# Four blocks of 448 tokens in layer 1, and 512s and 384s in layer 2, of an attention and two-layer MLP kernel

## The chip, the cores and the metric

The kernel runs on one core of one Trainium2 chip. The metric is the device time of one execution in microseconds, the median of several runs. Before the change it is 988.56 us (three runs, 987.62 to 990.99).

## What is computed

Attention over q, k and v of shape (4, 8, 576, 64), as the sum of two parts, then two dense layers over the 2304 tokens with 512 features each:

```python
q_d, k_d, v_d = (t.reshape(B, H, 144, 4, D).mean(axis=3) for t in (q, k, v))
out_up = np.repeat(sm_attn(q_d, k_d, v_d), 4, axis=2)
scores = np.where(abs(pos[:, None] - pos[None, :]) < 4, q @ k.T / 8, -1e9)
x = (out_up + softmax(scores) @ v), as (2304, 512)
h = x @ moe_w_in;   y = (h * sigmoid(1.702 * h)) @ moe_w_out
h = y @ moe2_w_in;  out = where(h > 0, h, exp(min(h, 0)) - 1) @ moe2_w_out
```

The four weight matrices are 512 x 2048 or 2048 x 512 and come as 64-bit floats.

## The kernel before, in words

Every large product is made of three: each operand is split into a high and a low part of the type fp32r, and high x high, high x low and low x high are added up in PSUM.

**Weights.** A layer has 32 weight tiles, `wi0` to `wi15` (the 16 column blocks of w_in) and `wo0` to `wo15` (the 16 row blocks of w_out). `load_w` (L129, the DMAs of L136 and L141 on SP's queue) brings one tile of 512 KB, 64-bit numbers. `conv_w` turns it into high and low parts: ACT L158, DVE L165 (twice, or once and ACT L168 for some tiles of layer 1), DVE L171, ACT L178 (the high part), DVE L182 (the low part). `Weights.convert` (L222) does one call's worth: the low part of one tile, the high part of another, the first half of a third. `need` (L234) forces conversions that are not yet done when a tile is about to be used.

**Layer 1** takes the tokens in the blocks of BLOCKS1. `tiles_of(blk)` is 512 // columns, so a block of 256 columns takes two of the 16 tiles of w_in a step (8 steps), a block of 512 one (16 steps). A step is `products_h1` (L755, 12 matmuls for each of its tiles, then the chain ACT L776 tanh, DVE L779, ACT L780 high part, DVE L781 low part) and, two steps later (LAG), `products_y1` (L789, 12 matmuls per tile into the y tiles in PSUM). On a block's last step the y tiles are copied out by ACT L810 into places of the tag `g`, of which there are two and which h's chain uses too, and stored to `ydram` by SP (L811): four `ye` tiles for a block of 512, two for one of 256. From block 2 on, a new block first splits its x (L299, L300), then finishes the y steps that wait, then begins with three h's. There are two places in PSUM for h.

**Attention** is cut into pieces that stand in a queue; `attend` (L727) emits one. In the loop over the steps (L994) one piece follows each chunk of matmuls (four a step), and a block whose inputs are not ready takes pieces until they are (L997).

**Layer 2** takes blocks of 512 tokens, the last of 256. Step s is `hidden2` (L935): 12 matmuls of `products_h2`, the chain ACT L921, ACT L922, DVE L924, ACT L929, DVE L931, one `convert` and on every fourth step a second. `products_o2` (L954) for the step two earlier follows: for each 128 tokens three matmuls of 512 columns. The first two steps of layer 2 stand beside the last two y steps of layer 1. On a block's last step ACT L970 and DVE L972 copy o out and SP stores it (L973). The rows of y of the next block are loaded by `load_y` (L887) and split by `split_y` (L892) in steps 8 to 13.

**Layer 2's weights.** After step 0 of the last block of layer 1 the attention's memory is free and the second `Weights` begins (L1056). Its first six tiles have places of their own; the others take the places of layer 1's tiles in the order of `released` (L982), as these have been read for the last time: `used` names the places that are free. In the last block of layer 1 a step calls `convert` once after its second chunk, and once more after its third chunk when the step's number is odd (L1030). Steps are counted from 0; the last block has the numbers 64 to 71. Its step 1 has two chunks, the steps from 2 on four.

Of the kernel before, what the change touches and what calls it, by code (L numbers as in the profile page):

```python
# [26 lines left out]
NF = 16  # L27
NK = 4
NSUM = 4

BLOCKS1 = [(0, 256), (256, 256), (512, 512), (1024, 512), (1536, 512), (2048, 256)]

XBUFS = 2
NEG = -1.0e9
# [21 lines left out]
LAG = 2  # L56
# [10 lines left out]
def kernel(  # L67
# [23 lines left out]
    NT = B * S  # L91
    NBLK = len(BLOCKS1)
    PSUM = bass.MemoryType.PSUM
# [162 lines left out]
    @contextmanager  # L256
    def behind():
        with ExitStack() as stack:
            for ins in urgent.values():
                stack.enter_context(tc.issue_after(ins.ins))  # L260
            yield
# [19 lines left out]
    def x_tile(blk):  # L281
        if blk not in x32:
            x32[blk] = xin.tile([P, NK, BLOCKS1[blk][1]], F32, tag="x32", name=f"x32_{blk}", bufs=XBUFS)
        return x32[blk]

    def block_of(gw):

        return next(i for i, (t0, n) in enumerate(BLOCKS1) if t0 <= 64 * gw < t0 + n)

    def split_x(blk, c):  # L290
        if blk not in xsplit:

            n = BLOCKS1[blk][1]
            nb = 2 if blk == 0 else 1
# [12 lines left out]
    class Unit:  # L307
# [284 lines left out]
        def pv(self, w0, w1):  # L592
# [10 lines left out]
            while a < w1:  # L603
                gw = self.b * NWIN + a
                blk = block_of(gw)
                t0, n = BLOCKS1[blk]
                e = min(w1, a + (t0 + n) // 64 - gw)
# [116 lines left out]
    def ready(blk):  # L724
        return not due[blk]

    def attend():  # L727

        if deferred:
            deferred.pop(0)()  # L730
        if not queue:
            return False
        piece, ends = queue[0]
        if ends is not None and block_of(ends.b * NWIN + ends.w1 - 1) >= nsplit[0] // NK + XBUFS:
            return False
        queue.pop(0)
        piece()
        if ends is not None:
            for users in due.values():
                users.discard(ends)  # L740
        return True

    def split_some(blk):

        if blk < NBLK and nsplit[0] < NK * (blk + 1) and ready(blk):
            split_x(blk, nsplit[0] % NK)
            nsplit[0] += 1
# [3 lines left out]
    def tiles_of(blk):  # L751

        return 512 // BLOCKS1[blk][1]

# [34 lines left out]
    def products_y1(blk, st):  # L789
        nf, (t0, tb) = tiles_of(blk), BLOCKS1[blk]  # L790

        if st == 0:
            yps[blk] = [ypool.tile([P, nf, tb], F32, tag=f"y{i % 2}", name=f"y{i}_{blk}") for i in range(NK // nf)]
        gh, gl = hg.pop((blk, st))
        last = st == NF // nf - 1
        for m in range(NK):
            n = 0
            for i in range(nf):
                f = nf * st + i
                for wp, gp in ((0, gh), (0, gl), (1, gh)):  # L800
                    nc.tensor.matmul(  # L801
                        out=yps[blk][m // nf][:, m % nf, :],
                        lhsT=w_out(1, f, wp)[:, m, :], rhs=gp[:, i, :],
                        start=(st == 0 and n == 0 and m % nf == 0), stop=(last and n == 3 * nf - 1),
                        skip_group_check=True,
                    )
                    n += 1
            if last and m % nf == nf - 1:
                t = gpool.tile([P, nf, tb], F32, tag="g", name=f"ye{m // nf}_{blk}", bufs=2)
                nc.scalar.activation(out=t, in_=yps[blk][m // nf], func=AF.Copy, scale=0.5)  # L810
                nc.sync.dma_start(  # L811
                    out=ydram[m - nf + 1:m + 1, :, t0:t0 + tb].rearrange("c p t -> p c t"), in_=t
                )
            if m % 2 == 1:
                yield
# [30 lines left out]
    kd, f = spare.pop(0)  # L846
# [30 lines left out]
        steps += [catch.pop(0), ahead.pop(0)]  # L877
    steps += catch + [(blk, st) for blk in range(2, NBLK) for st in range(NF // tiles_of(blk))]

    blocks = [(t, min(512, NT - t)) for t in range(0, NT, 512)]  # L880
    steps2 = [(bi, f) for bi in range(len(blocks)) for f in range(NF)]
    x2 = {}
    y32 = {}
# [3 lines left out]
    def load_y(bi, c):  # L887
        t0, n = blocks[bi]
        y32[bi, c] = x2pools[0].tile([P, 512], F32, tag="y32", name=f"y32_{bi}_{c}", bufs=2)
        nc.sync.dma_start(out=y32[bi, c][:, :n], in_=ydram[c, :, t0:t0 + n])  # L890
# [44 lines left out]
    def hidden2(s):  # L935
        bi, f = steps2[s]
        wt2.need("i", f)
        low_part = products_h2(s)
        if bi + 1 < len(blocks):
            if 8 <= f < 8 + NK:  # L940
                load_y(bi + 1, f - 8)
            if 10 <= f < 10 + NK:
                split_y(bi + 1, f - 10)
        wt2.load(AHEAD + wt2.half - wt2.loaded)
        with behind():
            wt2.convert()
        low_part()
        if s % 4 == 3:
            with behind():
                wt2.convert()  # L950
# [24 lines left out]
    wt2 = None  # L975
# [4 lines left out]
    order2 += [("o", f) for f in range(NF - 4, NF)]  # L980

    released = []  # L982
    for f2 in range(8 + LAG):
        released += [f"wi{f}" for f in (2 * f2, 2 * f2 + 1) if f < NF]
        released += [f"wo{f}" for f in (2 * (f2 - LAG), 2 * (f2 - LAG) + 1) if f >= 0]
    used = set()

    def rate(si):
        if due[1] and si < 8:
            return RATE0  # L990
        return RATE1

    waiting, prev = [], None
    for si, (blk, f2) in enumerate(steps + [(None, None)] * LAG):  # L994
        chunks = []
        if blk is not None:
            while not ready(blk):  # L997
                assert attend()
            if blk > 1 and f2 == 0:

                for _ in range(NK):
                    split_some(blk)
                while waiting:
                    prev = waiting.pop(0)
                    wt1.need("o", tiles_of(prev[0]) * (prev[1] + 1) - 1)
                    chunks.append(products_y1(*prev))
            while nsplit[0] < NK * (blk + 1):
                split_some(blk)
            wt1.need("i", tiles_of(blk) * (f2 + 1) - 1)
            chunks.append(products_h1(blk, f2))  # L1010
            waiting.append((blk, f2))
            if blk == NBLK - 1:
                used |= {f"wi{2 * f2}", f"wi{2 * f2 + 1}"}
        if len(waiting) > LAG or blk is None:
            prev = waiting.pop(0)
            wt1.need("o", tiles_of(prev[0]) * (prev[1] + 1) - 1)
            chunks.append(products_y1(*prev))
        if blk is None:
            hidden2(si - len(steps))
        nchunk = 0  # L1020
        for chunk in chunks:
            for _ in chunk:
                if not wt1.finished() and blk == 0:
                    wt1.convert()
                for _ in range(rate(si)):
                    attend()
                if blk == 0:
                    split_some(1)
                nchunk += 1
                if wt2 is not None and nchunk in (2, 3) and (nchunk == 2 or si % 2):  # L1030
                    wt2.load(AHEAD + wt2.half - wt2.loaded)
                    with behind():
                        wt2.convert()
        if blk == NBLK - 1:
            if 1 <= f2 <= NK:
                load_y(0, f2 - 1)
            if 3 <= f2 < 3 + NK:
                split_y(0, f2 - 3)
        if chunks and prev is not None and prev[0] == NBLK - 1:
            used |= {f"wo{2 * prev[1]}", f"wo{2 * prev[1] + 1}"}  # L1040
        if wt1.finished() and stage1 is not None:
            ls1.close()
            stage1 = None
        if not queue and nsplit[0] == NK * NBLK and l1a is not None:
            l1a.close()
            l1x.close()
            l1s.close()
            hpools.append(ls2.enter_context(tc.tile_pool(name="hpool2", bufs=2, space=PSUM, side="right")))
            l1a = None
            stage2 = ls2.enter_context(tc.tile_pool(name="stage2", bufs=1, side="right"))  # L1050
            x2pools.append(ls2.enter_context(tc.tile_pool(name="x2a", bufs=1, side="right")))
            wextra = ls2.enter_context(tc.tile_pool(name="wextra", bufs=1, side="right"))
            for i, tile2 in enumerate(order2):
                places[(2, *tile2)] = (wextra, f"we{i}") if i < NEXTRA else (wpool, released[i - NEXTRA])
            used |= {f"we{i}" for i in range(NEXTRA)}
            wt2 = Weights(2, order2, stage2, 3, lambda tag: tag in used, 0)  # L1056
            wt2.load(AHEAD)
# [9 lines left out]
    for s in range(LAG, len(steps2) + LAG):  # L1067
        if s < len(steps2):
            hidden2(s)
        f = steps2[s - LAG][1]  # L1070
# [34 lines left out]
```

## Time and profile before

| | |
|---|---|
| median of three runs | 988.56 us |
| profiled execution, span from first to last instruction | 1196.4 us (no other time of it is given) |
| granted TensorE clock of that execution, mean | 0.750 |
| matmuls (PE) busy | 1183.7 us, 99% |
| DVE busy | 503.3 us, 42% |
| ACT busy | 471.7 us, 39% |
| POOL busy | 102.0 us, 9% |

One execution is profiled; its span is longer than the runs that were only timed. PE is TensorE's matmuls, PEld its weight loads, DVE is VectorE, ACT ScalarE, SP the engine whose queue issues most DMAs. A row of a group of instructions gives line, engine, operation, tiles (out<-in), shape and count, then busy time in us, the mean of one in ns, and idle time before them with what ended it. In the order of time a row gives start and duration in us, and in brackets the idle time before it. Matmul durations overlap, so the pace is read from starts. `L766` and `L801` are h and y of layer 1, `L914` and `L963` h and o of layer 2.

### The profile page before, as it was taken

What the parts mean: (1) busy time and instruction counts of PE and PEld (TensorE: products, weight loads), DVE (VectorE), ACT (ScalarE), POOL (GpSimd) and SP (SyncE); (2) the same over time, 40 slices, a digit from 0 to 9 for tenths busy, and PEclk for the clock granted to TensorE, in tenths of its full rate; (3) what the DMA queues carried; (4) which work ended last, traced back from release to release, by engine and by line L of the source; (5) the groups of instructions that cost most, each with busy time, mean ns of one, the idle gap of its engine ahead of it and who ended that gap; (6) DMA issues with size and microseconds to landing.
All of it is one profiled execution on the core that took longest, in us unless ns stands there. A gap on an engine that the chain in (4) does not pass through costs nothing.

```text
span 1196.4 us, 15208 instructions
## 1 busy us (share of the span) xinstructions
PE 1183.7 (99%) x6028; PEld 881.7 (74%) x6028; DVE 503.3 (42%) x898; ACT 471.7 (39%) x1116; POOL 102.0 (9%) x117
## 2 busy tenths in 40 slices
PE   9999999999999999999999999999999999999998
PEld 4578999976667677777668986677767777676787
DVE  3777785344453442122122796673213222221222
ACT  5888654233332441122113464553223222322233
POOL 4243210211230000000000000000000000000000
PEclk8777777776777777777777777777777777777777
DMA  9668612332331102100004940001001000100000
GB/s 194 157 157 225 145 27 39 68 58 34 47 52 23 43 16 74 44 3 33 1 1 128 315 156 0 1 14 58 1 1 35 27 1 1 44 0 1 1 36 18
DMA packets 128822, 68.04 MB, mean 57 GB/s; under 512 B 99184, under 2 KB 118768, under 8 KB 128752
## 3 DMA queue, kind: packets, MB, share of 16 engines
q1 hardware_dynamic: 109040, 63.21, 18.9%
q0 software_dynamic: 14976, 2.69, 2.7%
q10 hardware_dynamic: 4736, 1.18, 0.6%
q8 instruction: 47, 0.77, 0.3%
q14 instruction: 23, 0.19, 0.1%
HBM read 57.59 MB, written 9.44 MB: 56 GB/s over the span
## 4 chain that ended last, share of the span: by engine, by line
PE 97%; ACT 2%; DVE 1%; issue 0%; DVEq 0%; ACTq 0%
PE h L766 22%; PE y L801 21%; PE o L963 21%; PE h L914 20%; PE busy L853 3%; PE qk L468 2%; PE pv L598 2%; PE ptr L572 2%; PE qkd L495 1%; PE pvd L582 1%; PE pdt L560 1%; PE pt L421 1%; ACT pd L525 0%; DVE wst1i L165 0%; ACT sl L518 0%
## 5 line engine op out<-in xcount | busy, mean ns | idle before, releaser
L801 PE MATMUL y<-g1h,whl1o 128*128 128x256 f32 (+1 forms) x768 | 253.3, 401 | 0.0
L963 PE MATMUL o<-whl2o,g2h 128*128 128x512 f32 x576 | 214.1, 457 | 0.0
L766 PE MATMUL h<-xh,whl1i 128*128 128x256 f32 (+1 forms) x768 | 209.6, 406 | 0.3 <-ACT xh L299 0.3
L914 PE MATMUL h<-x2h,whl2i 128*128 128x512 f32 (+1 forms) x640 | 190.9, 427 | 0.0
L801 PEld LDWEIGHTS y<-g1h,whl1o 128*128 128x128 f32 x768 | 154.6, 217 | 35.6 <-issue 3.4
L766 PEld LDWEIGHTS h<-xh,whl1i 128*128 128x128 f32 x768 | 143.1, 219 | 35.2 <-issue 3.0
L924 DVE SCALAR_TENSOR_TENSOR g<-e,h 128x512 f32<-128x512 f32 (+1 forms) x80 | 50.7, 634 | 262.8 <-ACT e L922 262.6
L914 PEld LDWEIGHTS h<-x2h,whl2i 128*128 128x128 f32 x640 | 122.9, 201 | 45.6
L801 PE MATMUL y<-g1l,whl1o 128*128 128x256 f32 (+1 forms) x384 | 152.5, 397 | 0.0
L963 PEld LDWEIGHTS o<-whl2o,g2h 128*128 128x128 f32 x576 | 113.7, 199 | 46.5
L921 ACT ACTIVATE e<-h 128x512 f32<-128x512 f32 (+1 forms) x80 | 44.5, 556 | 252.2 <-PE h L914 252.2
L963 PE MATMUL o<-whl2o,g2l 128*128 128x512 f32 x288 | 131.7, 457 | 0.0
L776 ACT ACTIVATE g<-h 128x512 f32<-128x512 f32 x72 | 42.8, 596 | 202.2 <-PE h L766 200.6
L779 DVE SCALAR_TENSOR_TENSOR g<-g,h 128x512 f32<-128x512 f32 x72 | 49.1, 685 | 174.4 <-ACT g L776 174.4
L766 PE MATMUL h<-xl,whl1i 128*128 128x256 f32 (+1 forms) x384 | 107.5, 403 | 0.0
L380 POOL DMA_DIRECT2D vd<-in_v_dram x72 | 84.7, 1238 | 243.0 <-DMA vd<-in_v_dram 181.0
L914 PE MATMUL h<-x2l,whl2i 128*128 128x512 f32 (+1 forms) x320 | 95.7, 427 | 0.0
L801 PEld LDWEIGHTS y<-g1l,whl1o 128*128 128x128 f32 x384 | 83.8, 218 | 15.1 <-issue 0.3
L766 PEld LDWEIGHTS h<-xl,whl1i 128*128 128x128 f32 x384 | 72.9, 224 | 15.4 <-issue 2.0
L914 PEld LDWEIGHTS h<-x2l,whl2i 128*128 128x128 f32 x320 | 61.1, 201 | 21.7
L963 PEld LDWEIGHTS o<-whl2o,g2l 128*128 128x128 f32 x288 | 57.6, 200 | 23.9
L931 DVE TENSOR_TENSOR g2l<-g,g2h 128x512 fp32r<-128x512 f32 (+1 forms) x80 | 51.6, 645 | 36.7 <-ACT g2h L929 36.2
(110 smaller groups left out, 1185.6 us busy)
## 6 DMA issues: line engine op xcount, KB each, us to landing
wst1i<-in_moe_w_in_dram SPq DMA_DIRECT2D x16, 512.0 KB
wst1o<-in_moe_w_out_dram SPq DMA_DIRECT2D x16, 512.0 KB
wst2i<-in_moe_w_in_dram SPq DMA_DIRECT2D x16, 512.0 KB
wst2o<-in_moe_w_out_dram SPq DMA_DIRECT2D x16, 512.0 KB
ydram<-ye SPq DMA_DIRECT2D x18, 256.0 KB
out_dram<-ot SPq DMA_DIRECT2D x18, 256.0 KB
y<-ydram SPq DMA_DIRECT2D x16, 256.0 KB
vw<-in_v_dram SPq DMA_DIRECT2D x24, 122.5 KB
```

Of the source, the lines that this page charges most:

```text
L380: nc.gpsimd.dma_start(out=self.vd[:, :, j, :], in_=src, accum_op=ALU.add)
L468: nc.tensor.matmul(out=ps[r, w - a, :], lhsT=self.qkT[0][r, 64 * w:64 * w + 64], rhs=self.qkT[1][r, ks:ks + KW], start=not by_pe, stop=Tru ...
L766: nc.tensor.matmul(out=ph[:, i, :], lhsT=w_in(1, f, c, wp), rhs=xp[:, c, :], start=(n == 0), stop=(n == 3 * NK - 1),)
L776: nc.scalar.activation(out=g, in_=ph, func=AF.Tanh, scale=0.851)
L779: nc.vector.scalar_tensor_tensor(out=g, in0=g, scalar=1.0, in1=ph, op0=ALU.add, op1=ALU.mult)
L801: nc.tensor.matmul(out=yps[blk][m // nf][:, m % nf, :], lhsT=w_out(1, f, wp)[:, m, :], rhs=gp[:, i, :], start=(st == 0 and n == 0 and m % ...
L853: ins = nc.tensor.matmul(out=busy.rearrange("p a b -> p (a b)")[:, :n], lhsT=ones[:, :P], rhs=ones[:, :n], start=True, stop=True)
L914: nc.tensor.matmul(out=ph[:, :n], lhsT=w_in(2, f, c, wp), rhs=xp[:, c, :n], start=(i == 0), stop=(i == 3 * NK - 1),)
L921: nc.scalar.activation(out=e[:, :n], in_=ph[:, :n], func=AF.Relu, scale=-1.0)
L924: urgent["dve"] = nc.vector.scalar_tensor_tensor(out=g[:, :n], in0=e[:, :n], scalar=-1.0, in1=ph[:, :n], op0=ALU.add, op1=ALU.max)
L931: return lambda: nc.vector.tensor_tensor(out=gl[:, :n], in0=g[:, :n], in1=gh[:, :n].bitcast(F32), op=ALU.subtract)
L963: nc.tensor.matmul(out=ops[bi][i], lhsT=gp[:, i * P:(i + 1) * P], rhs=wo[wp], start=(f == 0 and m == 0), stop=(f == NF - 1 and m == 2),)
```

## The change

The last four blocks of layer 1 have 448 columns each in place of 512, 512, 512 and 256; layer 2 has three blocks of 512 and two of 384 in place of four of 512 and one of 256. As `tiles_of(448)` is 1, the last block of layer 1 has 16 steps of one tile and not 8 of two, so the places of layer 1's weights come free one `wi` and one `wo` a step, and `convert` is called once a step there, never twice.

```diff
-BLOCKS1 = [(0, 256), (256, 256), (512, 512), (1024, 512), (1536, 512), (2048, 256)]
+BLOCKS1 = [(0, 256), (256, 256), (512, 448), (960, 448), (1408, 448), (1856, 448)]
+BLOCKS2 = [(0, 512), (512, 512), (1024, 512), (1536, 384), (1920, 384)]
...
-    blocks = [(t, min(512, NT - t)) for t in range(0, NT, 512)]
+    blocks = BLOCKS2
...
-    for f2 in range(8 + LAG):
-        released += [f"wi{f}" for f in (2 * f2, 2 * f2 + 1) if f < NF]
-        released += [f"wo{f}" for f in (2 * (f2 - LAG), 2 * (f2 - LAG) + 1) if f >= 0]
+    for st in range(NF + LAG):
+        released += [f"wi{st}"] if st < NF else []
+        released += [f"wo{st - LAG}"] if st >= LAG else []
...
             if blk == NBLK - 1:
-                used |= {f"wi{2 * f2}", f"wi{2 * f2 + 1}"}
+                used.add(f"wi{f2}")
...
-                if wt2 is not None and nchunk in (2, 3) and (nchunk == 2 or si % 2):
+                if wt2 is not None and nchunk == 2:
                     wt2.load(AHEAD + wt2.half - wt2.loaded)
                     with behind():
                         wt2.convert()
...
         if chunks and prev is not None and prev[0] == NBLK - 1:
-            used |= {f"wo{2 * prev[1]}", f"wo{2 * prev[1] + 1}"}
+            used.add(f"wo{prev[1]}")
```

## Rows read from the trace of the kernel before

**Rows 1.** The page: busy time of the engines, granted clock by slice, chain that ended last

```profile
PE 1183.7 (99%) x6028; PEld 881.7 (74%) x6028; DVE 503.3 (42%) x898; ACT 471.7 (39%) x1116; POOL 102.0 (9%) x117
...
PEclk8777777776777777777777777777777777777777
...
PE 97%; ACT 2%; DVE 1%; issue 0%; DVEq 0%; ACTq 0%
```

**Rows 2.** Stages of the span (columns in the first line)

```profile
core 0: us, PE busy (x) PEld busy (x) DVE busy (x) ACT busy (x) POOL busy (x), PEclk, DMA share, GB/s
...
294.00:430.00 136.00, 136.00 (x805) 93.62 (x805) 59.01 (x115) 47.34 (x159) 20.33 (x18) 0.75 0.21 38
...
539.00:648.00 109.00, 109.00 (x386) 76.38 (x385) 24.64 (x38) 24.00 (x42) 0.00 (x0) 0.75 0.05 15
648.00:713.00 65.00, 65.00 (x423) 62.01 (x422) 50.04 (x79) 34.72 (x60) 0.00 (x0) 0.75 0.78 262
713.00:820.00 107.00, 107.00 (x379) 74.95 (x378) 70.76 (x113) 53.67 (x90) 0.00 (x0) 0.75 0.04 10
820.00:1131.00 311.00, 311.00 (x1098) 217.90 (x1097) 70.47 (x106) 91.61 (x151) 0.00 (x0) 0.75 0.04 14
```

**Rows 3.** PE in order of time, 1131 to 1134 us

```profile
1131.36 0.74 PE L914 MATMUL h<-x2h,whl2i 128*128 128x256 f32 x4
...
1133.06 0.74 PE L963 MATMUL o<-whl2o,g2h 128*128 128x512 f32 x2
...
1133.91 0.74 PE L963 MATMUL o<-whl2o,g2h 128*128 128x512 f32 x2
```

**Rows 4.** PE in order of time, 685.4 to 685.7 us, single matmuls of 256 columns

```profile
685.38 0.32 PE L801 MATMUL y<-g1h,whl1o 128*128 128x256 f32 x1
685.50 0.32 PE L801 MATMUL y<-g1l,whl1o 128*128 128x256 f32 x1
685.65 0.47 PE L801 MATMUL y<-g1h,whl1o 128*128 128x256 f32 x2
```

**Rows 5.** Groups of DVE instructions, 648 to 713 us

```profile
L165 DVE TENSOR_SCALAR wst2i<-wst2i 128x512 uint16<-128x512 uint16 x18 | 13.5, 762 | 0.1
L165 DVE TENSOR_SCALAR wst2o<-wst2o 128x512 uint16<-128x512 uint16 x10 | 7.6, 756 | 0.0
L171 DVE SCALAR_TENSOR_TENSOR ww2i<-ww2i,wst2i 128x512 int32<-128x512 int32 x8 | 5.6, 706 | 0.4
L182 DVE TENSOR_TENSOR whl2i<-ww2i,whl2i 128x512 fp32r<-128x512 f32 x8 | 5.6, 705 | 0.0
```

**Rows 6.** PE in order of time, 787 to 791 us

```profile
787.49 1.32 PE L963 MATMUL o<-whl2o,g2h 128*128 128x512 f32 x4
...
790.90 0.47 PE L963 MATMUL o<-whl2o,g2h 128*128 128x512 f32 x1
```

**Rows 7.** DVE in order of time, 789 to 818 us

```profile
789.59 0.68 DVE L182 TENSOR_TENSOR whl2o<-ww2o,whl2o 128x512 fp32r<-128x512 f32 x1
...
816.84 0.69 DVE L182 TENSOR_TENSOR whl2o<-ww2o,whl2o 128x512 fp32r<-128x512 f32 x1
```

**Rows 8.** Two stretches of layer 2's first block, columns as in rows 2

```profile
695.60:716.40 20.80, 20.80 (x100) 16.83 (x99) 20.13 (x34) 14.73 (x26) 0.00 (x0) 0.75 0.50 175
716.40:800.00 83.60, 83.60 (x297) 58.58 (x296) 55.64 (x89) 40.81 (x69) 0.00 (x0) 0.75 0.00 0
```

**Rows 9.** All engines in order of time, entries into the fifth and sixth block

```profile
539.75 1.09 ACT L810 ACTIVATE ye<-y 128x512 f32<-128x512 f32 x2 [1.67 <-DMA ydram<-ye]
...
647.93 0.74 PE L766 MATMUL h<-xh,whl1i 128*128 128x256 f32 x4
...
653.24 0.69 DVE L779 SCALAR_TENSOR_TENSOR g<-g,h 128x512 f32<-128x512 f32 x1
```

**Rows 10.** Waits, 300 to 475 us: the longest of PE and its weight loads

```profile
PEld pv L598 <- issue: 2.9, 6, 0.5
```

**Rows 11.** SP's queue in order of time, the last loads of layer 2's weights

```profile
695.35 1.97 SPq L141 DMA_DIRECT2D wst2o<-in_moe_w_out_dram  x4
```

## The prediction, made before the changed kernel was built or run

> **What bounds the kernel now.** I read the page first, then stages, then single instructions. The page [rows 1] shows TensorE (PE) busy 99% of a 1196.4 us span, the chain that ended last 97% on PE, and a granted clock of 6 to 8 tenths of 2.4 GHz in every slice (0.75 in all stages of [rows 2]), between its two levels of 1.2 and 2.4 GHz. By stage [rows 2] PE has no idle time in any stretch shown, while DVE and ACT are busy a quarter to three quarters. The pace of single matmuls [rows 3] says what PE is short of. In layer 2's last block, twelve 256-column matmuls start at 1131.36 and the next ones at 1133.06: 142 ns each. Three 512-column ones take 1133.91 - 1133.06 = 0.85 us: 283 ns each. Twice the columns, twice the time: in this execution PE is bound by columns alone, with nothing fixed per matmul.
>
> **The timed runs are another case.** The only time known of the profiled execution is its span; the median of the runs shown, 988.56 us, is 208 us shorter. The four large products (h and y of layer 1, h and o of layer 2) each move 2304 x 192 = 442,368 columns, 1.769 million in all; at 283 ns for 512 they take 978 us. The rest of the profiled span, 218 us, could not fit into the 11 us that 988.56 would leave, so the timed runs had a faster PE. If only the products ran faster, they had 771 us, a clock of about 0.95; if all shrank alike, 0.75 x 1196.4 / 988.56 = 0.91; with any stall in them, more, up to 1. DVE, ACT and DMA have the durations of the rows in both cases. So I make two sums: against the profiled execution, and against PE at 2.4 GHz, where the covers shrink to 0.75 of themselves.
>
> **Columns and matmul counts.** Layer 1 keeps six blocks of 192 h and 192 y matmuls, layer 2 five blocks of 192 h, and o depends on no block size. Columns and counts stay: 0 in the profiled execution. What goes are 384 + 192 = 576 matmuls of 256 columns (the sixth block of layer 1, h of the fifth of layer 2). At 2.4 GHz they could lie above their 107 ns, should the weight load beside each not fit. Lower end: proportional as in [rows 3], 0. Upper end: single 256-column matmuls start as near as 120 ns and 150 ns to each other [rows 4]; the short one would leave 13 ns, 576 x 13 = 7.5 us. The pace of [rows 3] is the mean of many, [rows 4] a pair, so I take 1 us gained. The Trainium skill (TensorE: Matmul & The Clock Gate, section "LDWEIGHTS (loading the stationary operand)") has a load cost its columns at 1.2 GHz, 107 ns for 128: an estimate that just fits under a 256-column matmul, so by it this term is 0 and the sum below 1 us smaller; no row here shows a load as the limit.
>
> **Conversions started before layer 2 (the main term).** Each weight tile costs DVE two L165, one L171 and one L182: 2 x 0.76 + 0.71 + 0.70 = 2.93 us [rows 5]. By the code, before: step 0 of the sixth block opens the conversion; steps 1 to 7 give one call each, steps 3, 5 and 7 a second, the two steps with layer 2's first h two each: 14 ([rows 5] have 28 L165, 14 tiles). Then steps 2 to 15 give 14 + 4 = 18: the 32nd comes exactly at the block's end. After: 15 + 4 = 19 before, so the 32nd comes at step 11. What that is worth at present: the last tiles are ready just in time. PE turns from h to o at 787.49 and wants a low part at 790.90 [rows 6]; that part's DVE instruction starts at 789.59 and lasts 0.68 [rows 7], ready at 790.27. From the end of h it took 2.78 us (ACT's two passes, DVE's two), under a cover of twelve matmuls, 3.41 us. The profiled execution gains 0. At 2.4 GHz the cover is 2.56 us, 0.22 short, some 0.25 with a semaphore; six tiles (the last at 816.84 [rows 7]) stand so: 1.5 us stall now, gone after, since the tiles are four steps early. If the clock is 0.92 or less it is 0.
>
> **DVE's backlog.** From 695.6 to 716.4, where layer 2's first h stands beside the last y, DVE is busy 20.13 of 20.80 us [rows 8]. At 2.4 GHz PE passes this in 15.6: DVE comes out 4.5 us late. The next stretch has 55.64 us of DVE work in 83.6, at 2.4 GHz in 62.7, so up to 7 us to catch up, if DVE need not idle for ACT. Bounds 0 and 4.5; I take half, 2.3 us now. After, the same calls remain in those steps, but a late tile has four steps of room, and the steps before are roomier: 2.93 + 1.2 for one 448-column step's own two passes = 4.1 us against 24 x 187 ns = 4.5. Gone.
>
> **What the change adds.** At the entry into the sixth block, the four ye stores go through the two g places, DMA share 0.78 over that stage [rows 2]; ACT's last ye copies wait, and DVE's L779 on the first h ends at 653.24 + 0.69 = 653.93, 6.0 us after the block's first matmul at 647.93 [rows 9]. The third h needs that place in PSUM. Two h's cover 6.8 us now, 5.1 at 2.4 GHz, and 4.5 with 448 columns: 0.6 us more. The entry into layer 2 gets four ye in place of two; in the row at 539.75 a ye waits 1.67 us for a store [rows 9]. Between 0 and that, against a cover of twelve h matmuls of 2.56 us: 0.4 us. The extra steps (80 against 72 in layer 1) add ACT and DVE work off the path.
>
> **Cost nothing:** attention pieces are given out by step, and blocks 2 to 4 keep 16 steps, so the same pieces lie in 1/8 fewer columns of blocks 2 and 3; the longest sum of waits for weight loads in 300 to 475 us is 2.9 us and PE itself waits for nothing [rows 10], DVE is busy 59 of 136 us [rows 2]. If that cover were gone, the price is 2 x 64 x 384 columns, 20 us. Releasing places one tile a step: SP waits only for PE's last reader, and the last weight loads are issued at 695.35 [rows 11], 120 us before the last conversion; slower release still leaves them early. On SP's queue y loads and ye stores stand behind those loads; they move with them. Layer 2's tail: 384 ends with three o tiles in place of two, the last copy and store unchanged. At 448 or 384 columns the ACT and DVE chain of a step is shorter in proportion.
>
> **Sum.** Profiled execution: 0, a span of 1196.4 us again at that clock. Timed, with PE at 2.4 GHz: columns -1, conversions in time -1.5, backlog -2.3, the two entries +0.6 and +0.4, in all -3.8: 988.6 - 3.8 = 984.8 us. A measurement of this kernel can tell about 0.3%, 3.0 us, from no change.
>
> **Rivals.**
> 1. *Nothing shows.* The timed clock is near 0.91, or DVE catches up by itself; then every cover holds as in the trace. For it: no PE wait after 475 us. 988.6 us. That places freed singly feed loads that are early anyway is part of this case. Chance 0.33.
> 2. *The short matmuls were bound by their loads.* The 120 ns of [rows 4] is the floor: 7.5 in place of 1 us, 978.3. Against: exact proportion in [rows 3]. Chance 0.14.
> 3. *Slower: the ye stores at a block's entry.* Entries into the three later 448 blocks all go as the one at 648 and PE waits 6.0 - 4.5 = 1.5 us at each, less the 0.9 paid today: +3.6, and DVE's terms bring nothing: 992.2. It decides once DMA is as busy at the other entries as at 648; at 539.75 the ye waited as long, but DMA's share in 539 to 648 is 0.05. Chance 0.15.
>
> **Numbers.** Forecast 984.8 with chance 0.38; with rival 2, faster 0.52; same 0.33; slower 0.15. The range goes from somewhat below rival 2 to near rival 3: 976 to 991.5. The forecast's own goes from 981.6 (the whole backlog of 4.5 gained, nothing added) to 988.4 (none of it, 2.3 us added).
>
> **What would show it.** Right: in a profile at a clock near 1, waits of PE for L182 around layer 2's steps 11 to 15 in the kernel before and none after; the last L182 some five steps ahead of the last o of block 0; 448-column matmuls at 7/8 of the 512's pace. At 0.75, equal spans within 1 us or two. Wrong: PE waiting for L779 or ydram stores at block entries, for ACT in 300 to 475 us, or 256-column matmuls of the first two blocks well above half of 512's time.

## The result, and the profile after

The changed kernel takes 995.34 us (median of five runs, 993.99 to 996.79) where the kernel before took 988.56: a ratio of 1.0057, 95% interval 1.0039 to 1.0075. It is slower by some 0.6%, on the other side of the forecast of 984.8, and above the whole range.

The changed kernel's profiled execution took 996.79 us, 1.8 us beyond its span. The page, in the parts that answer to [rows 1]:

```profile
span 995.0 us, 15254 instructions
...
PE 963.9 (97%) x6028; PEld 825.8 (83%) x6028; DVE 504.2 (51%) x917; ACT 472.6 (48%) x1135; POOL 101.0 (10%) x117
...
PEclk9899899997999999999999999999999999999999
```

The granted clock is 0.98 here, against 0.75 in the execution of [rows 1] and [rows 2]. So the two cannot be set side by side. The first experiment was therefore the kernel before once more, for a profile at the same clock.

> The kernel before, unchanged, for a profile at the clock of the timed runs. Theory A (the cost lies in layer 1's four 448 blocks: entries into blocks, less cover for attention): a span near 987 us at a clock of 0.98, and in the stretch from block 2 to the first o of layer 2 some 5 us less than the changed kernel needs for it. Theory B (the cost lies in layer 2's 384 blocks): layer 1's stretch equal within 1 us and layer 2's 4 us or more shorter than in the changed kernel. The prediction's terms, which would have made the changed kernel faster: waits of PE for L182 near the end of layer 2's first block, about 1.5 us, and DVE late by 2 us after layer 2's first h.

It gave a span of 991.8 us at a clock of 0.98, and 993.7 us for that run (the kernel before, timed beside it, had a median of 989.78). Every comparison below is with this trace. I cut both at three points that any of the kernels has: the first y matmul of layer 1's third block, the first h of layer 2, and the 384th h matmul of layer 2 (the end of its second block). Up to the first point the attention and the first two blocks run; in two kernels of this study that are the same up to there (the unchanged one and the one with more calls in layer 2) it lies at 245.4 and at 237.7 us, so that part is left out. Stages A, B and C of the unchanged kernel (columns in the first line):

```profile
core 0: us, PE busy (x) PEld busy (x) DVE busy (x) ACT busy (x) POOL busy (x), PEclk, DMA share, GB/s
245.44:578.25 332.81, 331.61 (x2080) 275.05 (x2078) 144.80 (x253) 121.19 (x308) 20.33 (x18) 1.00 0.26 73
578.25:758.64 180.39, 176.42 (x782) 143.55 (x780) 108.58 (x172) 91.73 (x152) 0.00 (x0) 0.99 0.10 33
758.64:991.84 233.20, 229.51 (x1094) 191.49 (x1092) 67.82 (x113) 88.12 (x162) 0.00 (x0) 1.00 0.06 21
```

The same of the changed kernel:

```profile
243.81:584.94 341.13, 339.30 (x2102) 302.51 (x2100) 167.30 (x300) 132.35 (x338) 20.40 (x18) 1.00 0.28 76
584.94:758.96 174.02, 172.94 (x757) 141.65 (x755) 93.81 (x146) 83.94 (x141) 0.00 (x0) 1.00 0.07 23
758.96:995.02 236.06, 230.71 (x1094) 200.28 (x1092) 67.02 (x112) 88.52 (x163) 0.00 (x0) 0.99 0.06 21
```

Stage A, layer 1's four wide blocks, is 8.3 us longer. Stage B, the entry into layer 2 with the conversions, is 6.4 us shorter. Stage C, the rest of layer 2, is 2.9 us longer. Sum: +4.8 us. A gain came where one was forecast, and more of it than forecast (what made it, below); what went wrong lies in the stages where the prediction had costed the change at about nothing.

**Where stage A goes.** The pace of PE's matmuls, read from their starts. The unchanged kernel in layer 1's fourth block, h and y of 512 columns:

```profile
400.40 1.07 PE L766 MATMUL h<-xh,whl1i 128*128 128x512 f32 x4
...
405.84 1.07 PE L766 MATMUL h<-xh,whl1i 128*128 128x512 f32 x4
```

The changed one in its fourth block, and then in its last, where layer 2's weights are loaded and converted beside it:

```profile
401.33 0.97 PE L767 MATMUL h<-xh,whl1i 128*128 128x448 f32 x4
...
420.79 0.97 PE L767 MATMUL h<-xh,whl1i 128*128 128x448 f32 x4
...
520.47 0.99 PE L767 MATMUL h<-xh,whl1i 128*128 128x448 f32 x4
...
579.99 0.99 PE L767 MATMUL h<-xh,whl1i 128*128 128x448 f32 x4
```

Between the starts of the three pairs lie 24, 96 and 288 matmuls. So one of 512 columns takes 5.44 / 24 = 226.7 ns, one of 448 takes 19.46 / 96 = 202.7, in the last block 59.52 / 288 = 206.7. At 2.4 GHz the columns alone are 213.3 and 186.7 ns. A matmul here has some 13 ns beside its columns, and at 448 it has 16, or 20 in the last block of this execution. For 256 columns the pace is 120.0 (below): 106.7 + 13.3. The number of matmuls is the same, 1536 in the four blocks. Before: 1152 x 0.2267 + 384 x 0.1200 = 307.2 us. After, with 202.7 for all: 311.3, which is +4.1; the last block's 206.7 on all of it but its last two y steps, 360 matmuls, adds 1.4. **+5.5 us** where the prediction had -1. At 202.7 a width of 448 is dearer per column than 512.

The rest of stage A: the entry into the sixth block, where PE waits for DVE's first pass on h [rows 9]. Waits of PE from 475 to 580 us, the unchanged kernel:

```profile
PE h L766 <- DVE g L779: 1.2, 1, 1.2
```

and the changed one:

```profile
PE h L767 <- DVE g L780: 1.8, 1, 1.8
```

That is +0.6 us. Two parts of the 1536 matmuls lie outside the stage and are gains there: the 36 h's ahead of the first cut (36 x 24.0 ns, 0.9) and the last two y steps behind the second (0.9, below). So stage A itself holds 5.5 + 0.9 + 0.9 = 7.3 of pace and 0.6 of entry; 0.4 of its 8.3 is left for the other entries and the attention.

### The profile page after: what moved, and what is told of

The parts are those of the page before. It is cut to its first block, busy times and chain, and to the rows that moved or that the text cites. A ratio compares the mean times of both kernels' runs of the same rounds, so it can differ in the third digit from the quotient of the medians.

```text
span 995.0 us, 15254 instructions
## 1 busy us (share of the span) xinstructions
PE 963.9 (97%) x6028; PEld 825.8 (83%) x6028; DVE 504.2 (51%) x917; ACT 472.6 (48%) x1135; POOL 101.0 (10%) x117
## 4 chain that ended last, share of the span: by engine, by line
PE 82%; DVE 7%; ACT 7%; DMA 2%; issue 1%; SPq 0%; DVEq 0%; ACTq 0%
PE o L964 20%; PE h L915 19%; PE h L767 18%; PE y L802 17%; PE pv L599 1%; PE qk L469 1%; PE ptr L573 1%; PE pvd L583 1%; PE qkd L496 1%; ACT wst1o L169 1%; DVE wst1o L166 1%; PE pdt L561 1%; DMA y<-ydram 1%; ACT sl L519 1%; ACT pd L526 1%
## 5 line engine op out<-in xcount | busy, mean ns | idle before, releaser
L802 PE MATMUL y<-g1h,whl1o 128*128 128x448 f32 (+1 forms) x768 | 213.9, 345 | 0.0
L964 PE MATMUL o<-whl2o,g2h 128*128 128x512 f32 x576 | 178.7, 391 | 1.1 <-ACT ye L811 1.1
L767 PE MATMUL h<-xh,whl1i 128*128 128x448 f32 (+1 forms) x768 | 174.5, 349 | 4.4 <-ACT xh L300 2.5
L915 PE MATMUL h<-x2h,whl2i 128*128 128x512 f32 (+1 forms) x640 | 159.4, 371 | 0.0
L802 PE MATMUL y<-g1l,whl1o 128*128 128x448 f32 (+1 forms) x384 | 130.4, 340 | 0.0
L964 PE MATMUL o<-whl2o,g2l 128*128 128x512 f32 x288 | 112.8, 392 | 0.0
L777 ACT ACTIVATE g<-h 128x448 f32<-128x448 f32 (+1 forms) x80 | 44.3, 556 | 137.1 <-PE h L767 134.6
L780 DVE SCALAR_TENSOR_TENSOR g<-g,h 128x448 f32<-128x448 f32 (+1 forms) x80 | 50.5, 632 | 113.3 <-ACT g L777 113.2
L767 PE MATMUL h<-xl,whl1i 128*128 128x448 f32 (+1 forms) x384 | 88.7, 346 | 0.6 <-DVE xl L301 0.6
L930 ACT ACTIVATE g2h<-g 128x512 fp32r<-128x512 f32 (+1 forms) x80 | 47.1, 589 | 45.5 <-DVE g L925 45.2
```

Source lines behind the costliest of these rows:

```text
L767: nc.tensor.matmul(out=ph[:, i, :], lhsT=w_in(1, f, c, wp), rhs=xp[:, c, :], start=(n == 0), stop=(n == 3 * NK - 1),)
L777: nc.scalar.activation(out=g, in_=ph, func=AF.Tanh, scale=0.851)
L780: nc.vector.scalar_tensor_tensor(out=g, in0=g, scalar=1.0, in1=ph, op0=ALU.add, op1=ALU.mult)
L802: nc.tensor.matmul(out=yps[blk][m // nf][:, m % nf, :], lhsT=w_out(1, f, wp)[:, m, :], rhs=gp[:, i, :], start=(st == 0 and n == 0 and m % ...
L915: nc.tensor.matmul(out=ph[:, :n], lhsT=w_in(2, f, c, wp), rhs=xp[:, c, :n], start=(i == 0), stop=(i == 3 * NK - 1),)
L930: nc.scalar.activation(out=gh[:, :n], in_=g[:, :n], func=AF.Copy)
```

## The experiments

**Which half costs.** One kernel with layer 1 of the changed kernel (its blocks, the single releases, one call a step) and layer 2 as before, one with only layer 2's new blocks:

```diff
-BLOCKS1 = [(0, 256), (256, 256), (512, 512), (1024, 512), (1536, 512), (2048, 256)]
+BLOCKS1 = [(0, 256), (256, 256), (512, 448), (960, 448), (1408, 448), (1856, 448)]
...
-                if wt2 is not None and nchunk in (2, 3) and (nchunk == 2 or si % 2):
+                if wt2 is not None and nchunk == 2:
```

```diff
-    blocks = [(t, min(512, NT - t)) for t in range(0, NT, 512)]
+    blocks = BLOCKS2
```

> Layer 1 with the four blocks of 448 and places freed one a step; layer 2 with blocks of 512 and a last one of 256 as before. Theory A: ratio to the kernel before 1.004 to 1.008, all of the loss. Theory B: 0.998 to 1.002.

> Layer 1 as before; layer 2 with three blocks of 512 and two of 384. Theory A: ratio to the kernel before 0.998 to 1.002. Theory B: 1.003 to 1.008.

Layer 1 alone: 993.1 us, ratio 1.003 (1.0015 to 1.0045). Layer 2 alone: 993.07, ratio 1.0029 (1.0014 to 1.0044). Neither theory had both halves cost the same; they do, and their sum is the whole within the intervals. The stages of layer 1 alone:

```profile
245.69:586.93 341.24, 339.33 (x2101) 303.49 (x2100) 167.42 (x300) 132.35 (x338) 20.33 (x18) 0.99 0.29 76
586.93:760.95 174.02, 172.94 (x756) 141.63 (x755) 93.89 (x146) 83.90 (x141) 0.00 (x0) 1.00 0.08 24
760.95:994.52 233.57, 229.52 (x1094) 191.44 (x1092) 67.78 (x113) 88.16 (x162) 0.00 (x0) 1.00 0.06 21
```

and of layer 2 alone:

```profile
243.56:576.65 333.09, 331.82 (x2079) 275.06 (x2078) 145.04 (x253) 121.16 (x308) 20.36 (x18) 1.00 0.26 73
576.65:756.78 180.13, 176.47 (x782) 143.47 (x780) 108.31 (x172) 91.65 (x152) 0.00 (x0) 0.99 0.10 32
756.78:992.45 235.67, 230.71 (x1094) 200.26 (x1092) 67.04 (x112) 88.50 (x163) 0.00 (x0) 1.00 0.06 21
```

A and B belong to layer 1's part, to 0.1 us. Of C's 2.9 us layer 2's part alone has 2.5; layer 1's alone has 0.4, which comes up again with the tail.

**Is it the width?** The changed kernel with the old widths in another order, the 256 as fifth block and a 512 as last (the reordered kernel from here on). That keeps the last block at 16 steps, with the single releases and one call a step; layer 2 as before:

```diff
-BLOCKS1 = [(0, 256), (256, 256), (512, 448), (960, 448), (1408, 448), (1856, 448)]
+BLOCKS1 = [(0, 256), (256, 256), (512, 512), (1024, 512), (1536, 256), (1792, 512)]
...
-    blocks = BLOCKS2
+    blocks = [(t, min(512, NT - t)) for t in range(0, NT, 512)]
```

> Layer 1's last four blocks 512, 512, 256, 512, so that the last block has 16 steps of one tile and frees places singly as in the changed kernel, while no block has 448 columns; layer 2 in blocks of 512 and a last one of 256. Width theory (a 448-column matmul costs more per column than one of 512; the early conversions are a gain of 6 us): the products of layer 1 cost what they did before, the gain stays: ratio to the kernel before 0.993 to 0.997. Rival (the loss comes with the last block's 16 steps and its entry, whatever the width): 1.001 to 1.006.

982.38 us, ratio 0.9933 (0.9911 to 0.9954): faster than both kernels. Its stages:

```profile
237.72:569.68 331.96, 331.93 (x2103) 276.23 (x2102) 164.12 (x284) 128.20 (x320) 20.29 (x18) 1.00 0.29 78
569.68:744.33 174.65, 173.56 (x756) 141.63 (x755) 93.82 (x145) 84.22 (x141) 0.00 (x0) 1.00 0.07 25
744.33:977.53 233.20, 229.52 (x1094) 191.49 (x1092) 67.81 (x113) 88.23 (x162) 0.00 (x0) 1.00 0.06 21
```

It has the gain of stage B without the loss of A, and C is the old one. So the gain comes with a last block of 16 steps, and the loss with blocks of 448 columns, not from how places come free. Its fifth block has the pace of 256, 24 matmuls of y and then h:

```profile
456.05 0.28 PE L802 MATMUL y<-g1h,whl1o 128*128 128x256 f32 x1
...
458.93 0.64 PE L767 MATMUL h<-xh,whl1i 128*128 128x256 f32 x4
```

**Is it how 448 columns lie in memory?** The changed kernel with x's tiles laid out 512 wide and 448 of it used:

```diff
-            parts = [xpool.tile([P, nb, NK, n], F32R, tag=f"x{p}", name=f"x{p}_{blk}") for p in "hl"]
+            parts = [xpool.tile([P, nb, NK, 512 // nb], F32R, tag=f"x{p}", name=f"x{p}_{blk}")[:, :, :, :n] for p in "hl"]
```

> The changed kernel, with the x tiles of layer 1's 448 blocks laid out with 512 columns for each chunk, so that every chunk begins at a multiple of 2048 bytes; the g tiles stay packed. Layout theory: h matmuls of 448 columns come down from 203 ns to about 199 or 200 (448/512 of 227 ns), y stays at 203. Width theory: both stay at 203 ns.

994.26 us in its one run. The layout theory falls: 448 columns keep 202.5 ns (in the last block 24 matmuls from 559.67 to 564.53 us). That the last block has 202.5 here and 206.7 in the changed kernel does not come of the layout: layer 1 alone, with x's tiles as in the changed kernel, has 202.7 there too (below).

**Widths side by side**, 512, 448, 512 and 320 in one program, layer 2 with its new blocks:

```diff
-BLOCKS1 = [(0, 256), (256, 256), (512, 448), (960, 448), (1408, 448), (1856, 448)]
+BLOCKS1 = [(0, 256), (256, 256), (512, 512), (1024, 448), (1472, 512), (1984, 320)]
```

> The changed kernel with layer 1's last four blocks of 512, 448, 512 and 320 columns. Width theory: 512 at 227 ns and 448 at 203 in the same run, a block apart, and 320 near 320/2.4 plus 13 to 20 ns, 147 to 153 ns. If the pace hung on the place in the run instead, 512 and 448 would have equal time per column.

999.14 us. In this one execution the fourth, the fifth and the last block:

```profile
390.28 0.97 PE L767 MATMUL h<-xh,whl1i 128*128 128x448 f32 x4
...
395.14 0.98 PE L767 MATMUL h<-xh,whl1i 128*128 128x448 f32 x4
...
499.38 1.07 PE L767 MATMUL h<-xh,whl1i 128*128 128x512 f32 x4
...
502.10 0.39 PE L802 MATMUL y<-g1h,whl1o 128*128 128x512 f32 x1
...
531.00 0.75 PE L767 MATMUL h<-xh,whl1i 128*128 128x320 f32 x4
...
534.52 0.75 PE L767 MATMUL h<-xh,whl1i 128*128 128x320 f32 x4
```

448: 4.86 / 24 = 202.5 ns (0.01 us of reading is 0.4 ns here); 512: 2.72 / 12 = 226.7; 320: 3.52 / 24 = 146.7, which is 133.3 + 13.3. So 320 has what 256 and 512 have, and the extra 2.7 ns are 448's own. (384 in layer 2's last block has 176.7, 160 + 16.7.) What makes them, no run here shows. Nor is 512 the same everywhere: in the unchanged kernel eight h matmuls of layer 2's first block take 617.00 to 618.88 us, 235 ns each, and eight of its second 707.18 to 709.00, 227.5; the two blocks take x2 from different pools. The total is above the changed kernel's; PE waits 5.7 us for DVE's first pass in the last block, and o 5.5 us for ye.

**Do the conversions slow the last block?** None in it; all of them fall into layer 2:

```diff
-                if wt2 is not None and nchunk == 2:
+                if wt2 is not None and nchunk == 2 and blk is None:
```

> The changed kernel without the calls of convert in layer 1's last block (the loads stay); the same work is forced when layer 2 needs it. If the conversions (ACT and DVE) make the last block's matmuls slower, they go from 207 to 203 ns; if the loads do, they stay at 207. Layer 2's first block then waits for conversions: PE waits for L183, and a span longer by 15 to 45 us.

1067.29 us in its one run. The last block runs at 202.5 ns (24 matmuls from 559.67 to 564.53, as in the kernel with the padded x). But that does not show that conversions make 206.7, for layer 1 alone, with the same conversions and the same x, has 202.7 as well:

```profile
517.15 1.09 PE L767 MATMUL h<-xh,whl1i 128*128 128x448 f32 x4 [1.84 <-DVE g L780]
...
523.70 0.97 PE L767 MATMUL h<-xh,whl1i 128*128 128x448 f32 x4
...
582.07 0.97 PE L767 MATMUL h<-xh,whl1i 128*128 128x448 f32 x4
```

From 523.70 to 582.07 lie 288 matmuls: 202.7 ns. What layer 1 alone lost, it lost before that, behind the wait of 1.84 us at the block's entry (columns as in [rows 2]):

```profile
517.15:523.70 6.55, 6.55 (x24) 5.91 (x25) 5.22 (x9) 4.56 (x9) 0.00 (x0) 0.74 0.80 257
```

At a granted clock of 0.74, 24 matmuls take 6.55 us in place of 4.86: 1.7. The kernel with three places for ot (below), whose layer 1 is the changed kernel's, does the same. In the changed kernel's own profile the clock stayed 1.00 after the same wait, and the block ran at 206.7. Stage A is equal all the same: 341.1, 341.2, 341.1 and 341.0 us in the changed kernel, layer 1 alone, the padded one and the one with three places. Without conversions, after a wait of 1.55 us with the clock at 1.00, it is 339.5. So with the conversions the last block of 448 costs some 1.6 us more, in one of two forms; why one or the other stays open. In the reordered kernel the last block, 512 columns with the conversions beside them, stays at 226.7 and PE does not wait at its entry. The price of having no conversion before layer 2 is some 70 us: from 480 to 760 us PE waits 44.6 us for ACT's high parts, and from 600 to 700 the granted clock is 0.81.

**What stage B gained.** The unchanged kernel with more calls in layer 2, and nothing else:

```diff
-        if s % 4 == 3:
+        if s % 2 == 1:
```

> The kernel before, blocks of both layers unchanged; only layer 2's extra conversion call falls on every odd step in place of every fourth, so that the 32nd call comes at step 13 of the first block, not 15. If late low parts cost the first block of layer 2 its 3 us (theory A), the weight loads' waits for DVE's low part (1.9 us, five times, in the unchanged kernel) go and block 0's steps from 8 on shorten by 2 to 3 us: a median 986 to 987.5 beside 989.6. If DVE's backlog at the entry into layer 2 is the cost (theory B), two more calls in steps 3 to 7 deepen it: o's wait of 3.6 us for the ye copies stays or grows, and the median is 989.5 to 992.

989.15 us beside 990.01, ratio 0.9992 (0.9978 to 1.0005): no difference. The waits say why. Unchanged kernel, 540 to 720 us, PE and its weight loads:

```profile
PE o L963 <- ACT ye L810: 3.6, 1, 3.6
...
PEld o L963 <- DVE whl2o L182: 1.9, 5, 0.8
```

With more calls (no row for L182 is left):

```profile
PE o L963 <- ACT ye L810: 3.9, 1, 3.9
```

Counted from layer 2's first h, its 133rd o comes at 81.90 us in place of 80.48, 1.42 later, and its 205th at 115.23 in both. The late low parts had cost 1.42 us, and those go; with the one extra call that falls into layer 2's first two steps the entry costs 1.42 more. Half of that lies before the first o (18.68 us after the first h in place of 17.97) and half in the twelve o's after it, at the lower clock, so that the two are equal is chance. Both theories were half of it.

The other way round, the reordered kernel with a second call on odd steps of the last block, 26 calls before layer 2:

```diff
-                if wt2 is not None and nchunk == 2:
+                if wt2 is not None and nchunk in (2, 3) and (nchunk == 2 or si % 2):
```

> The kernel with 256 columns as fifth block and 512 as last (e3_256_fifth), with a second conversion call on the odd steps of the last block of layer 1: seven calls more before layer 2, 26 in place of 19. If one call a step was early enough (theory A), nothing shows: 981.5 to 983.5, with before at 989.6. If DVE's load in the first steps of layer 2 still costs (theory B), the first block of layer 2 loses its calls from step 6 on and ends 0.5 to 2 us earlier: 980.5 to 982. If conversions slow TensorE's pace in layer 1's last block (theory C; 207 in place of 203 ns in the changed kernel), the 384 matmuls of that block go from 227 to 229 or 231 ns: 0.8 to 1.5 us more, 983 to 984.

994.58 us, ratio 1.0043 (1.0028 to 1.0059): none of the three; 12 us are lost. PE's wait for ACT's ye copies at the first o of layer 2 is 8.5 us (1.1 in the reordered and in the changed kernel). On ACT the ye copies, which free the PSUM that o takes, stand behind the conversions and behind what waits for DVE's:

```profile
596.20 0.67 ACT L159 ACTIVATE ww2i<-wst2i 128x512 f32<-128x512 f32 x1
597.31 0.68 ACT L159 ACTIVATE ww2o<-wst2o 128x512 f32<-128x512 f32 x1 [0.44 <-DVE whl2i L183]
597.88 1.24 ACT L811 ACTIVATE ye<-y 128x512 f32<-128x512 f32 x2
...
601.81 0.58 ACT L811 ACTIVATE ye<-y 128x512 f32<-128x512 f32 x1
```

And the wait costs more than its length. After it PE ran at the lower clock:

```profile
602.45 1.22 PE L964 MATMUL o<-whl2o,g2h 128*128 128x512 f32 x2 [8.47 <-ACT ye L811]
603.47 0.63 PE L964 MATMUL o<-whl2o,g2l 128*128 128x512 f32 x1
...
604.75 0.63 PE L964 MATMUL o<-whl2o,g2l 128*128 128x512 f32 x1
```

and by stretch, columns as in [rows 2]:

```profile
602.40:608.00 5.60, 5.55 (x13) 4.39 (x14) 4.55 (x8) 2.68 (x5) 0.00 (x0) 0.50 0.14 50
```

Three o matmuls from 603.47 to 604.75 take 427 ns each, 512 / 1.2, and the granted clock in that stretch is 0.50. The same stands after the unchanged kernel's 3.6 us, in the 4.4 us from o's first start:

```profile
596.20:600.60 4.40, 4.38 (x12) 3.53 (x13) 4.26 (x7) 3.18 (x6) 0.00 (x0) 0.61 0.19 63
```

Its first twelve o's start 4.46 us before what follows them, where a later twelve take 2.75: 1.7 us. In the changed kernel, after 1.1 us of wait, the clock stayed:

```profile
602.40:608.00 5.60, 5.53 (x24) 4.52 (x25) 5.07 (x10) 3.95 (x8) 0.00 (x0) 1.00 0.13 44
```

What shortened the wait from 3.6 to 1.1 us is PE's order. The first h after layer 1's last y, and the first o, in the unchanged kernel:

```profile
589.48 1.08 PE L914 MATMUL h<-x2h,whl2i 128*128 128x512 f32 x4
...
596.22 1.22 PE L963 MATMUL o<-whl2o,g2h 128*128 128x512 f32 x2 [3.63 <-ACT ye L810]
```

and in the changed one:

```profile
595.30 1.09 PE L915 MATMUL h<-x2h,whl2i 128*128 128x512 f32 x4
...
602.47 0.73 PE L964 MATMUL o<-whl2o,g2h 128*128 128x512 f32 x2 [1.08 <-ACT ye L811]
```

In the first pair 13 h matmuls stand from the one row to the other, in the second 26. The copies that o waits for come no earlier to speak of: counted from layer 2's first h, the first o starts at 17.97 us in the unchanged kernel, at 17.54 in the changed one and at 17.96 in the reordered one, where 25 h's stand before it. So the wait is shorter because PE has another step's h to do first. The code gives both kernels the same order of h and o; what changed it in the trace, no run shows.

Last, the reordered kernel with fewer calls at the entry:

```diff
         wt2.load(AHEAD + wt2.half - wt2.loaded)
-        with behind():
-            wt2.convert()
+        if s >= LAG:
+            with behind():
+                wt2.convert()
```

> The kernel with 256 columns as fifth block and 512 as last (e3_256_fifth), without the conversion calls that stand in layer 2's first two steps beside layer 1's last y: 17 calls before layer 2 in place of 19, the 32nd at step 13 of its first block, not 11. If conversion calls at the entry are what o waits behind (theory A), the wait of o for the ye copies (1.1 us) goes, and from layer 2's first h to its 132nd o it takes 74.9 to 75.2 us in place of 76.2; the low parts at step 13 are in time: a median 981 beside 982.4, with before at 989.7. If the ye copies and stores alone make that wait (theory B), it stays at 1.1 and the time at 982.4. If two calls fewer already make low parts late (theory C), PE or its weight loads wait for them after layer 2's step 11 and up to 1.4 us are lost there: 982.5 to 984.

983.63 us, ratio 0.9939 (0.9915 to 0.9964); the reordered kernel had 0.9933 (0.9911 to 0.9954), and the timed runs can't tell the two apart. The traces can: the 133rd o comes 74.95 us after the first h, not 76.16, the first at 16.28, not 17.96, PE has no wait left from 540 to 720 us, and none for low parts. Theory A holds in the traces, with 1.2 us.

**The tail.** The changed kernel with a third place for the output tile:

```diff
-                t = g2pool.tile([P, 512], F32, tag="ot", name=f"ot{i}_{bi}")
+                t = g2pool.tile([P, 512], F32, tag="ot", name=f"ot{i}_{bi}", bufs=3)
```

> The changed kernel, with three places for the output tile ot in place of two. If the third copy of a 384 block waits for a store of the same block (theory A), the wait of 2.16 us before the last ACT copy goes, and from the start of the last o matmul to the end it takes 4.0 to 4.3 us as in the unchanged kernel (5.7 in the changed one): a span 1.5 us shorter, 993.5. If the longer tail comes from three stores sharing the queue (theory B), it stays at 5.3 to 5.7 us and only the idle time moves from ACT to the store.

ACT's last copy in the changed kernel:

```profile
991.11 0.60 ACT L971 ACTIVATE ot<-o 128x512 f32<-128x512 f32 x1 [2.16 <-DMA out_dram<-ot]
```

and with three places:

```profile
985.93 0.60 ACT L971 ACTIVATE ot<-o 128x512 f32<-128x512 f32 x1 [0.76 <-PE o L964]
```

From the start of the last o matmul to the end: 4.08 us in the unchanged kernel, 5.74 in the changed one, 4.46 with three places. 1.3 of the 1.7 us were the third copy's wait for the first tile's store. The other 0.4 is no matter of three tiles: layer 1 alone, whose last block has two, takes 4.44. 991.75 us in its one run.

## Why the prediction was wrong

**"Columns and matmul counts" is the step that failed.** It took -1 us, between 0 and -7.5. Measured: +5.5 in layer 1 (4.1 from the pace of 448 alone) and, for 384 columns in layer 2's h, what is left of stage C's 2.9 beside the tail, some +1.2. It looked only at the 256s that go and gave the 448s and 384s the pace of their columns, because [rows 3] show exact proportion. But that was a TensorE at 0.75: 142 and 283 ns there, 120 and 226.7 at full clock. Whatever takes the 13 ns at full clock is hidden at 0.75; at half the clock (427 ns above) nothing is left over either. A proportion read at 0.75 was carried to the clock of the timed runs, while the covers had been rescaled with care. The Trainium skill (TensorE: Matmul & The Clock Gate, section "Wait — 56ns, not 53.3ns?") has a fixed cost per matmul that only shows at 2.4 GHz, which these traces bear out; it gives some 2.5 ns, where 13 to 17 are measured here, each matmul with a weight load of its own. Even so, a fixed cost would have left the sum as it was, since the number of matmuls does not change. It is that the cost differs by width, 2.7 ns more for 448, that no row of before could show, and the bounds had excluded a loss. Why it differs stays open.

**"Conversions started before layer 2", -1.5: right** in size and cause. The waits for L182 are there in the unchanged kernel and gone after; the run with more calls puts them at 1.42 us. The last low part starts at 662.6 in the changed kernel, 684.0 in the unchanged one.

**"DVE's backlog", -2.3: a gain is there, but not by this mechanism.** From layer 2's first h to the steady steps stage B gained 6.4 us in all: 1.4 for the low parts; about 0.9 for the last two y steps, which hold 24 matmuls of 448 in place of 48 of 256 (24 x 0.2027 = 4.9 against 48 x 0.120 = 5.8); the other 4.1 at the entry. There o's wait for the ye copies fell from 3.6 to 1.1 us, 2.5, and the 1.7 us at the lower clock went with it. That 2.5 is near the forecast 2.3 is luck: the first o came only 0.4 us earlier after layer 2's first h, and the wait fell because 13 more h matmuls stood before it. Conversions do press on that entry: in the reordered kernel the first o comes 1.7 us earlier without two of the calls, 8.2 later with seven more before layer 2. But from the unchanged to the changed kernel that is not what moved the wait. That PE's clock can fall after a wait the prediction did not have.

**"What the change adds"**: the entry into the sixth block was forecast at +0.6 and measured at +0.6 (1.8 for 1.2). It did not have the 1.6 us or so that go with the conversions in that block, as lower clock after the wait or as slower pace. The four ye at the entry into layer 2, +0.4, do not show beside the gain there.

**"Cost nothing"**: attention's cover held (no wait of PE from 300 to 475 us in either trace), and single releases cost nothing, as the reordered kernel shows. "The last copy and store unchanged" was wrong: three o tiles on two places put a store in the chain, +1.3 of the tail's 1.7.

**Sum of the steps**, as measured: in stage A +7.3 for the pace, +0.6 for the entry and +0.4, -6.4 in B, +2.9 in C, in all +4.8 in one pair of traces; the medians differ by 6.8, and their interval is 3.9 to 7.4 us.

**The rivals.** The second fell, though its 120 ns is what a 256-column matmul takes at full clock: that is its columns and 13 ns, the same 13 as at 512, so it is no floor of the short ones. The third had the sign, and a time 3 us short, but not the cause: PE's waits at entries into layer 1's blocks grew by 0.6 us, not 3.6, and stage B brought more than DVE's terms. The first assumed a clock near 0.91 in the timed runs; they show 0.98.

## What to carry to other kernels

Before the widths of blocks are changed at equal count, read the pace of each width at the clock of the timed runs; a trace at a lower clock hides the part of a matmul that is not columns. Here an order of the old widths, with 512 last, kept the gain (982.4 us) that widths of 448 gave back. Work that is moved ahead of a bottleneck's entry is only free until the copies that release that entry stand behind it, and a wait of TensorE there can be paid again at half the clock. And a pace seen in one execution is first compared with another of the same code: the last block's 206.7 ns did not come back in two kernels with the same layer 1.

## What was not expected of the hardware

- Beside its columns an fp32r matmul with its own weight load took 13.3 ns at 256 and 320, 13.4 at 512, 16.0 at 448 and 16.7 at 384 columns, at the granted clock of 1.00; nothing at 0.50 (427 ns for 512). With x2 from the one pool 512 columns in layer 2 took 235 ns, from the other 227.5.
- In layer 1's last block 448 columns took 206.7 ns in one execution, and 202.7 in two others with the same layer 1. The cause is open.
- After a wait of 3.6 us the granted clock of PE was 0.61 in the next 4.4 us, after one of 8.5 us 0.50 in the next 5.6; after 1.1 us it stayed 1.00. After one of 1.8 us it was 0.74 over the next 24 matmuls in layer 1 alone, and 1.00 in the changed kernel: the same wait went either way.
